# Router logits taken out of bursts and into the last walk of a feed-forward, in a fused attention and two-feed-forward kernel

## The chip, the cores and the metric

The kernel runs on one core of a Trainium2 chip. The metric is device time in microseconds (us) of one execution; lower is better. Three runs of the kernel before gave 2235.82, 2237.16 and 2239.37 us, with the median at 2237.16.

## What is computed

```python
# 1. attention: q, k, v of [4, 8, 576, 64], masked by blocks of 64, softmax, times v
x = attn.transpose(0, 2, 1, 3).reshape(2304, 512)
# 2. first feed-forward, d_ff 1536
xn = x / rms(x) * rms_g
x = (silu(xn @ w_gate) * (xn @ w_val)) @ w_out
# 3. second feed-forward, E = 8 experts of width 1024
logits = x @ gate                      # [2304, 8]
P = exp(logits - logits.max())
for _ in range(8):                     # the "normalisation"
    P /= P.sum(1, keepdims=True) + 1e-9
    P /= P.sum(0, keepdims=True) + 1e-9
    P *= 2304 / 8
out = sum(P[:, e:e+1] * (relu(x @ w1[e]) @ w2[e]) for e in range(8))
```

Everything is float32. The large products are made of three fp32r matmuls each (high times high, high times low, low times high part), so operands are split beforehand: a copy rounds to the high part, a subtraction gives the low part.

## The kernel before

**Order of the work.** The kernel does not issue instructions as it is written. Each piece of work is recorded with `G.op` (engine, estimated duration, function, buffers read and written, priority). `Graph.emit` then schedules all of it: 12 rounds of a forward list schedule and a backward pass that gives each piece its time to the end as its next key, and the round with the earliest estimated end is issued. `lat` is the delay that the scheduler assumes from a piece to those that depend on it. Splits, copies and additions may have a second engine (`alts`), which the scheduler chooses between. So a change in one place can change keys, engines and order anywhere else. Real waits come from the buffers alone, not from the estimates.

**Attention** (lines 370 to 870) makes 32 heads; the first feed-forward's first blocks of tokens are scheduled in among them. Line 662 (ScalarE) or its alternative on line 664 (VectorE) divides the probabilities by their sums.

**First feed-forward** (`moe1`, `moe1_up`, `moe1_down`). Tokens form five blocks of 512, 512, 512, 384 and 384 (`BL`); a pass over the 12 pieces of d_ff for one block is called a walk here. For each piece `xw` (matmuls of line 896) gives gate and value, ScalarE, VectorE and GpSimdE make the hidden tile, and for each two pieces line 927 multiplies by `wo` into the result `acc[j]`, added up by VectorE (line 936). The token operands of a walk lie in the two `XT` tiles in turn; the two `T1` tiles hold temporaries of every piece.

**Second feed-forward** (`moe2`). `logits(j)`, line 1140, multiplies each 128 tokens of `acc[j]` by the gate, whose right side has only 8 columns: 4 float32 matmuls for each of 18 token tiles, recorded as 144 TensorE instructions since each runs as two. One block's logits are one piece of work, in the one PSUM bank of the ring `PO`, copied out to `lg` by ScalarE. `sink` makes P out of them: VectorE sums rows, TensorE sums over partitions with a matmul by ones (line 1182), VectorE scales columns, eight times over. `pass_operands` makes the token operands of the first pass, a Strassen-like scheme over `acc[0]` to `acc[2]`: differences of blocks (helper `add`, line 1062) into the ring `CT`, then splits (lines 294, 298 and 307) into the tiles `xs` and, for the 256-token part, into one `XT` tile. `CT` begins with the two `T1` tiles, which are free only when the first feed-forward is done, and goes on with four pieces of the tile `pad`. `up` and `down` are the products with w1 (line 1279) and w2 (line 1344); each expert has four groups `g`, and for the first expert P is not needed. `first_pass` runs the logits, the operands, and then the groups; `sink` stands after the first group.

Of the kernel before, what the change touches and what calls it, by code (L numbers as in the profile page):

```python
# [226 lines left out]
def t_mm(n):  # L227
    return max(n / 2.4, 107.0) + 2
# [7 lines left out]
def tile_attn_moe_moe2(ctx: ExitStack, tc: tile.TileContext, qT, kT, vP, wg, wv, wo, rg, gw, w1, w2, ident_d, mq_d, mk_d, bm_d, out):  # L236
# [651 lines left out]

    THREE = ((0, 0), (0, 1), (1, 0))
# [13 lines left out]
    def moe1_up(j, f, wgt, wvt, prio):  # L903
# [3 lines left out]
        xw(psg, wgt, x1[j], xv, n, 2.0)  # L907
        xw(psv, wvt, x1[j], xv, n, 2.0)
# [32 lines left out]
    def moe1():  # L941
        batches = attention()
        pend = None
        for j in range(NB):
            next(batches, None)
            for g in range(NF // 2):
# [9 lines left out]
                for f in fs:  # L956
                    a = get("g", f, wg[f])
                    b = get("v", f, wv[f])
                    hs.append(moe1_up(j, f, a, b, 2.0))
# [5 lines left out]

    GF = 2
    NG = NF2 // GF
    c_pool = []

    def late(make):  # L970

        box = []

        def get():
            if not c_pool:
                att_stack.close()
                c_pool.append(ctx.enter_context(tc.tile_pool(name="c1", bufs=1, side="right", reuse_waits="tile")))
            if not box:
                box.append(make(c_pool[0]))
            return box[0]  # L980

        return get

    def late_buf(make, par=False):
        b = Buf(late(make), par=par)
        b.before = set(att_ops)
        return b
# [28 lines left out]
    def moe2():  # L1016
# [12 lines left out]
        def cut(o, n):  # L1029
# [14 lines left out]
        gwr = late_buf(lambda p: p.tile([128, NK, E], F32, name="gwr"))  # L1044
        onec = late_buf(lambda p: p.tile([128, 128], F32, name="onec"))
        lg = late_buf(lambda p: p.tile([128, TT, E], F32, name="lg"), par=True)
# [18 lines left out]

        read_x = {(j, p): set() for j in range(NB) for p in range(2)}
# [62 lines left out]
        G.op("SP", 100, lambda: nc.sync.dma_start(out=gwr(), in_=gw), w=[gwr], lat=2000)  # L1129
        G.op("DVE", 100, lambda: nc.vector.memset(onec(), 1.0), w=[onec])  # L1130

        def logits(j):

            n, nt, t0 = BL[j], BL[j] // 128, B0[j] // 128
            ps = PO.next()

            def go():
                for t in range(nt):
                    for k in range(NK):
                        nc.tensor.matmul(out=ps()[:, E * t : E * t + E], lhsT=raw_x(j, 128 * t, k, 128), rhs=gwr()[:, k, :],  # L1140
                                         start=k == 0, stop=k == NK - 1)

            o = G.op("PE", 220 * NK * nt, go, r=[gwr, *accb[j]], w=[ps], prio=1.0)
            read_x[j, 0].add(o)
            read_x[j, 1].add(o)
            G.op("ACT", 150, lambda: nc.scalar.activation(
                out=lg()[:, t0 : t0 + nt, :], in_=ps()[:, 0 : E * nt].rearrange("p (t e) -> p t e", t=nt), func=AF.Copy),
                r=[ps], w=[lg])

        def sink():  # L1150

            V = nc.vector
            G.op("DVE", 300, lambda: V.tensor_reduce(out=sc1()[:, 0:1], in_=lg().rearrange("p t e -> p (t e)"), axis=AX, op=ALU.max),
                 r=[lg], w=[sc1])
# [458 lines left out]
```

## Time and profile before

| what | value |
|---|---|
| median of three runs | 2237.16 us |
| the profiled execution, its own time | 2237.22 us |
| its span, first to last instruction | 2234.7 us |
| TensorE busy | 2182.5 us, 98% of the span |
| VectorE, ScalarE, GpSimdE busy | 1467.0, 990.3, 1148.5 us |
| mean granted TensorE clock | 0.984 |

The span covers the instructions of the core; 2.5 us of the execution's time lie outside it. The granted clock is a share of full speed: 1.00 is 2.4 GHz and 0.50 is 1.2 GHz, and a value between is a stretch in which both occurred. Busy time of TensorE includes slow matmuls, so 98% busy does not mean 98% at full speed. In the tables PE is TensorE, PEld its weight loads, DVE VectorE, ACT ScalarE, POOL GpSimdE and SP the engine that issues the DMAs.

### The profile page before, as it was taken

What the parts mean: (1) busy time and instruction counts of PE and PEld (TensorE: products, weight loads), DVE (VectorE), ACT (ScalarE), POOL (GpSimd) and SP (SyncE); (2) the same over time, 40 slices, a digit from 0 to 9 for tenths busy, and PEclk for the clock granted to TensorE, in tenths of its full rate; (3) what the DMA queues carried; (4) which work ended last, traced back from release to release, by engine and by line L of the source; (5) the groups of instructions that cost most, each with busy time, mean ns of one, the idle gap of its engine ahead of it and who ended that gap; (6) DMA issues with size and microseconds to landing.
All of it is one profiled execution on the core that took longest, in us unless ns stands there. A gap on an engine that the chain in (4) does not pass through costs nothing.

```text
span 2234.7 us, 31371 instructions
## 1 busy us (share of the span) xinstructions
PE 2182.5 (98%) x10974; PEld 1870.0 (84%) x10974; DVE 1467.0 (66%) x2455; ACT 990.3 (44%) x2134; POOL 1148.5 (51%) x1050
## 2 busy tenths in 40 slices
PE   8798899999999999999999999999999999999999
PEld 6676678887899989999999999999888888888887
DVE  7889967666632577655555555555667777777665
ACT  6789667575311354333343333344342323233332
POOL 6456732321411565556656565565465546454554
PEclk9699999999999999999999999999999999999999
DMA  6556666553677455554555555455565566656563
GB/s 166 178 169 201 192 231 217 164 162 114 208 252 228 142 176 193 192 190 170 176 182 189 184 190 183 170 173 186 202 222 192 188 206 197 196 190 209 192 202 113
DMA packets 159025, 418.16 MB, mean 187 GB/s; under 512 B 22282, under 2 KB 50762, under 8 KB 158868
## 3 DMA queue, kind: packets, MB, share of 16 engines
q1 hardware_dynamic: 158868, 416.17, 56.2%
q8 instruction: 86, 1.41, 0.3%
q14 instruction: 71, 0.58, 0.1%
HBM read 275.00 MB, written 141.08 MB: 186 GB/s over the span
## 4 chain that ended last, share of the span: by engine, by line
PE 84%; DVE 4%; ACT 1%; issue 1%; POOL 0%; DVEq 0%; POOLq 0%; ACTq 0%
PE ps L1279 24%; PE pm L1344 19%; PE pm L1501 11%; PE pm L896 10%; PE pm L1279 7%; PE pm L927 5%; PE po L1501 3%; PE ps L672 1%; PE ps L487 1%; PE po L715 1%; PE po L1140 1%; DVE acc L356 0%; DVE acc L354 0%; DVE qa L461 0%; DVE acc L936 0%
## 5 line engine op out<-in xcount | busy, mean ns | idle before, releaser
L1279 PE MATMUL ps<-xs,w 128*128 128x384 f32 (+2 forms) x2478 | 508.3, 348 | 2.2 <-ACT xs L294 1.3
L1279 PEld LDWEIGHTS ps<-xs,w 128*128 128x128 f32 x2478 | 437.8, 189 | 47.8 <-ACT xs L294 1.7
L896 PE MATMUL pm<-x,w 128*128 128x512 f32 (+1 forms) x1440 | 335.7, 379 | 2.8 <-POOL w L307 1.3
L1359 DVE SCALAR_TENSOR_TENSOR acc<-pm,Pm,acc 128x512 f32<-128x512 f32 x280 | 210.0, 750 | 156.5 <-PE pm L1344 153.6
L896 PEld LDWEIGHTS pm<-x,w 128*128 128x128 f32 x1440 | 260.6, 192 | 35.3 <-POOL w L307 2.4
L1344 PE MATMUL pm<-w,h 128*128 128x512 f32 x1152 | 279.6, 391 | 0.0
L307 POOL TENSOR_TENSOR w<-raw,w 128x512 fp32r<-128x512 f32 (+1 forms) x156 | 194.2, 1254 | 126.7 <-ACT w L294 114.0
L1344 PEld LDWEIGHTS pm<-w,h 128*128 128x128 f32 x1152 | 210.2, 188 | 39.3
L1344 PE MATMUL pm<-w,x 128*128 128x512 f32 x768 | 187.4, 392 | 0.0
L307 POOL TENSOR_TENSOR h<-t,h 128x512 fp32r<-128x512 f32 (+1 forms) x61 | 74.4, 1219 | 199.9 <-ACT h L294 179.4
L1344 PEld LDWEIGHTS pm<-w,x 128*128 128x128 f32 x768 | 143.0, 188 | 26.7
L927 PE MATMUL pm<-h,w 128*128 128x512 f32 (+1 forms) x720 | 163.9, 374 | 1.0 <-DVE h L307 0.5
L1482 DVE TENSOR_TENSOR acc<-pm,acc 128x512 f32<-128x512 f32 x169 | 116.5, 690 | 68.7 <-PE pm L1501 68.0
L927 PEld LDWEIGHTS pm<-h,w 128*128 128x128 f32 x720 | 129.7, 190 | 18.1 <-DVE h L307 1.0
L1279 PE MATMUL pm<-xs,w 128*128 128x256 f32 (+2 forms) x654 | 139.1, 336 | 0.0
L1293 DVE TENSOR_TENSOR pad<-ps,pad 128x384 f32<-128x384 f32 (+2 forms) x127 | 66.2, 522 | 104.6 <-ACT pad L1288 65.6
L1501 PE MATMUL pm<-x,w 128*128 128x512 f32 x510 | 126.5, 391 | 0.5 <-DVE x L307 0.5
L307 POOL TENSOR_TENSOR x<-pad,x 128x512 fp32r<-128x512 f32 (+1 forms) x71 | 92.3, 1302 | 67.4 <-ACT x L294 64.0
L1279 PEld LDWEIGHTS pm<-xs,w 128*128 128x128 f32 x654 | 111.9, 189 | 15.0
L1288 ACT ACTIVATE pad<-ps 128x256 f32<-128x256 f32 (+2 forms) x115 | 55.0, 478 | 145.1 <-PE ps L1279 145.0
L1288 ACT ACTIVATE t<-ps 128x384 f32<-128x384 f32 (+1 forms) x72 | 36.3, 504 | 181.8 <-PE ps L1279 179.1
L307 POOL TENSOR_TENSOR w<-pad,w 128x512 fp32r<-128x512 f32 x62 | 85.6, 1383 | 60.1 <-ACT w L294 55.6
(352 smaller groups left out, 4282.8 us busy)
## 6 DMA issues: line engine op xcount, KB each, us to landing
raw<-w_dram SPq DMA_DIRECT2D x128, 256.0 KB, 2.9
w<-kg SPq DMA_DIRECT2D x48, 512.0 KB, 4.4
w<-kv SPq DMA_DIRECT2D x48, 512.0 KB, 3.9
w<-ko SPq DMA_DIRECT2D x48, 512.0 KB, 4.2
fa<-w SPq DMA_DIRECT2D x32, 512.0 KB, 4.1
fd<-w SPq DMA_DIRECT2D x32, 512.0 KB, 3.9
sb<-w SPq DMA_DIRECT2D x32, 512.0 KB, 3.8
sc<-x SPq DMA_DIRECT2D x32, 512.0 KB, 2.6
```

Of the source, the lines that this page charges most:

```text
L307: eng.tensor_tensor(out=out_(), in0=a(), in1=b(), op=ALU.subtract)
L487: nc.tensor.matmul(out=ps()[:, o : o + n], lhsT=a[:, 128 * t : 128 * t + 128], rhs=c[:, k0 : k0 + n], start=start, stop=stop)
L672: A("PE", 109 if n > 64 else 58, lambda: nc.tensor.transpose(out=ps()[:, o : o + n], in_=p()[0:n, k0 : k0 + 128], identity=ident_t[0:n, 0:n]),
L896: nc.tensor.matmul(out=ps()[:, 0:n], lhsT=w()[:, a, 128 * k : 128 * k + 128], rhs=xv()[:, c, k, 0:n], start=k == 0 and (a, c) == (0, 0), s ...
L927: nc.tensor.matmul(out=ps()[:, 0:n], lhsT=wos[q]()[:, a, 128 * m : 128 * m + 128], rhs=ht()[:, c, 0:n], start=q == 0 and (a, c) == (0, 0), ...
L1279: nc.tensor.matmul(out=bank()[:, 0:n], lhsT=w()[:, a, o + 128 * k : o + 128 * k + 128], rhs=views[p, q, i, k, c](), start=start and k == 0 ...
L1288: G.op("ACT", t_act(n, True), lambda: nc.scalar.activation(out=t()[:, 0:n], in_=bank()[:, 0:n], func=AF.Copy), r=[bank], w=[t])
L1293: G.op("DVE", t_v1(n), lambda: nc.vector.tensor_tensor(out=t()[:, 0:n], in0=bank()[:, 0:n], in1=t()[:, 0:n], op=ALU.add), r=[bank, t], w=[t])
L1344: nc.tensor.matmul(out=y(), lhsT=hs[f][half]()[:, a, o : o + 128], rhs=ws[f]()[:, c, :], start=f == 0 and (a, c) == (0, 0), stop=f == GF - ...
L1359: G.op("DVE", 63 + t_v1(512), lambda y=y, dst=dst, tt=tt, e=e: nc.vector.scalar_tensor_tensor(out=dst(), in0=wide(y()), scalar=Pm()[:, tt, ...
L1482: G.op("DVE", t_v1(N), lambda: nc.vector.tensor_tensor(out=dst(), in0=bank()[:, 0:N], in1=dst(), op=ALU.add), r=[bank, dst], w=[dst])
L1501: nc.tensor.matmul(out=bank()[:, 0:N], lhsT=w()[:, a, o : o + 128], rhs=ops[i][gi]()[:, c, 0:N], start=start and gi == 0 and (a, c) == (0, ...
```

## The change

Three things are changed. First, the router's gate is loaded and its PSUM bank taken at the start of the last walk, and the logits are made one matmul group at a time: 60 of the 72 (15 token tiles by 4) stand between the gate and value products of the last walk, from its second piece on; the other 12, of the last block, stand two at a time in the first group's 256-token product. One ScalarE copy takes all of them to `lg`. Second, the first pass's operands are recorded before the rest of `moe2` and use a ring `CT0` of eight pieces of `pad`, without the `T1` tiles. Third, in `sink` the assumed delays between VectorE and TensorE are 2000 ns and 300 ns in place of 130 ns and its VectorE estimates are longer, and the products with w2 of the first expert's last group are made to come, in the scheduler, after the last scaling of `sink`.

```diff
-    def xw(ps, w, x, xv, n, prio):
+    def xw(ps, w, x, xv, n, prio, more=()):
         for k in range(NK):
-            def go(k=k):
+            extra = more[k] if more else []
+            def go(k=k, extra=extra):
                 for a, c in THREE:
                     nc.tensor.matmul(
...
+                for t, k2 in extra:
+                    logit(t, k2)
-            G.op("PE", 3 * t_mm(n), go, r=[w, x[k]], w=[ps], prio=prio)
+            o = G.op("PE", 3 * t_mm(n) + 260 * len(extra), go, r=[w, x[k], *logit_reads(extra)], w=[ps, *logit_writes(extra)], prio=prio)
+            logit_done(o, extra)
...
+    def logit(t, k):
+
+        j = max(x for x in range(NB) if B0[x] <= 128 * t)
+        o = k * BL[j] + 128 * t - B0[j]
+        nc.tensor.matmul(out=router["ps"]()[:, E * t : E * t + E], lhsT=acc[j][:, o : o + 128], rhs=router["gw"]()[:, k, :],
+                         start=k == 0, stop=k == NK - 1)
...
         for j in range(NB):
             next(batches, None)
+            spots = [[] for _ in range(NF * 2 * NK)]
+            if j == NB - 1:
+                router["gw"] = late_buf(lambda p: p.tile([128, NK, E], F32, name="gwr"))
+                router["ps"] = PO.next()
+                G.op("SP", 100, lambda: nc.sync.dma_start(out=router["gw"](), in_=gw), w=[router["gw"]], lat=2000)
+                todo = [(t, k) for t in range(B0[j] // 128) for k in range(NK)]
+                first = 2 * NK
+                for i, x in enumerate(todo):
+                    spots[first + i * (len(spots) - first) // len(todo)].append(x)
...
-        CT = ring_of([*T1.tiles, *(cut(3072 + 384 * i, 384) for i in range(4))],
-                     [set().union(*(b.users for b in T1[-2:]))] * 2 + [atts] * 4)
-        SP_ = ring_of([cut(512 * i, 512) for i in range(4)], [atts] * 4)
+        CT0 = ring_of([*(cut(3072 + 384 * i, 384) for i in range(4)), *(cut(512 * i, 512) for i in range(4))], [atts] * 8)
...
+        xs0 = pass_operands(0, CT0)
+        diffs = atts.union(*(b.users for b in CT0))
+        CT = ring_of([*T1.tiles, *(cut(3072 + 384 * i, 384) for i in range(4))],
+                     [set().union(*(b.users for b in T1[-2:]))] * 2 + [diffs] * 4)
+        SP_ = ring_of([cut(512 * i, 512) for i in range(4)], [diffs] * 4)
...
-        def logits(j):
...
         def sink():
...
+            SLACK, BACK = 2000.0, 300.0
...
             for _ in range(8):
-                G.op("DVE", 1424, rows, r=[Pm], w=[Pm, sm1, sm8])
+                G.op("DVE", 1950, rows, r=[Pm], w=[Pm, sm1, sm8], lat=SLACK)
...
-                     r=[onec, sm8], w=[pc])
-                G.op("DVE", 665, lambda pc=pc: columns(pc), r=[pc, Pm], w=[Pm, sc1])
+                     r=[onec, sm8], w=[pc], lat=BACK)
+                last = G.op("DVE", 800, lambda pc=pc: columns(pc), r=[pc, Pm], w=[Pm, sc1], lat=SLACK)
...
+            return last
...
-                        G.op("PE", 3 * GF * t_mm(512), go, r=[hs[0][half], hs[1][half], *ws], w=[y], prio=2.0)
+                        G.op("PE", 3 * GF * t_mm(512), go, r=[hs[0][half], hs[1][half], *ws], w=[y], prio=2.0,
+                             after=early if (e, g) == (0, 3) else ())
...
-            for j in range(NB):
-                logits(j)
-            xs = pass_operands(0, CT)
+            xs = xs0
+            rest = [(t, k) for t in range(B0[NB - 1] // 128, TT) for k in range(NK)]
...
-                        hs = up(0, q, xs[q], w1s, CT, relu)
+                        hs = up(0, q, xs[q], w1s, CT, relu, rest if q else None)
...
-                        sink()
+                        early.add(sink())
```

`up` takes two entries of `rest` ahead of each of its products, as `xw` takes `more`; both record the tokens read, so that `acc` is not overwritten before. Lines move by 24 to 30 numbers: 896, 927, 1140, 1182, 1279 and 1344 of before are 920, 976, 935, 1202, 1304 and 1372 of the change.

**TensorE in the last walk.** The rows below are TensorE's order before, where the logits of the first block (`gwr` is the gate, `acc_61` the first block) come between two pieces; pm is the PSUM tile, x_84 the walk's tokens, w a weight tile, and x16 counts logit matmuls in a row.

```order
L927 MATMUL pm_89<-h_78,w_74 128x384 x3
L927 MATMUL pm_89<-h_79,w_66 128x384 x3
L1140 MATMUL po_96<-gwr,acc_61 128x8 x16
L896 MATMUL pm_90<-x_84,w_69 128x384 x12
L896 MATMUL pm_91<-x_84,w_70 128x384 x12
```

The same place with the change, from the walk's second piece on:

```order
L920 MATMUL pm_90<-x_84,w_69 128x384 x3
L935 MATMUL po_96<-gwr,acc_61 128x8
L920 MATMUL pm_90<-x_84,w_69 128x384 x3
L935 MATMUL po_96<-gwr,acc_61 128x8
L920 MATMUL pm_90<-x_84,w_69 128x384 x6
L935 MATMUL po_96<-gwr,acc_61 128x8
```

Sixteen logit matmuls in a row have become single ones, each between groups of three or six wide matmuls, and this pattern goes on through the walk.

**TensorE at the first rounds of `sink`.** Before, these are the rows from the matmul that spreads the maximum (line 1159) to the second matmul by ones (line 1182); xs and x_85 are token operands, sm the row sums.

```order
L1159 MATMUL po_96<-sc_6556,onec 128x1
L1279 MATMUL ps_93<-xs_5334,w_69 128x384 x6
L1182 MATMUL po_96<-sm_6609,onec 128x8
L1279 MATMUL ps_94<-xs_5291,w_69 128x256 x3
L1279 MATMUL ps_94<-x_85,w_69 128x256 x3
L1279 MATMUL ps_93<-xs_5280,w_70 128x384 x6
L1279 MATMUL ps_93<-xs_6510,w_68 128x384 x6
L1182 MATMUL po_96<-sm_6609,onec 128x8
```

With the change (1179 and 1202 are those two lines; 1372 is the product with w2):

```order
L1179 MATMUL po_96<-sc_6725,onec 128x1
L1304 MATMUL pm_92<-xs_5262,w_73 128x384 x6
L1304 MATMUL ps_95<-xs_5291,w_66 128x384 x6
L1304 MATMUL ps_93<-xs_5282,w_66 128x384 x6
L1372 MATMUL pm_89<-w_71,x_84 128x512 x3
L1372 MATMUL pm_89<-w_72,x_84 128x512 x3
L1304 MATMUL ps_95<-xs_5311,w_67 128x384 x6
L1372 MATMUL pm_90<-w_71,x_84 128x512 x3
L1372 MATMUL pm_90<-w_72,x_84 128x512 x3
L1202 MATMUL po_96<-sm_6805,onec 128x8
```

Ahead of the first matmul by ones stood 6 wide matmuls; now 36 stand there (24 of 384 columns, 12 of 512).

**VectorE in the attention.** This is a piece of the difference, around the normalisation of one head (rs holds the inverse sums, p the probabilities; lines 354 and 356 convert weights).

```order
-L664 TENSOR_SCALAR p_1_120<-p_1_120,rs_135 128x256
-L354 TENSOR_SCALAR acc_64<-acc_64 128x512
-L664 TENSOR_SCALAR p_1_126<-p_1_126,rs_135 128x576
-L356 SCALAR_TENSOR_TENSOR acc_64<-acc_64 128x512
-L911 SCALAR_TENSOR_TENSOR t_83<-t_83,pm_90 128x512
-L664 TENSOR_SCALAR p_1_122<-p_1_122,rs_135 128x384
```

These multiplications have left VectorE for ScalarE. Counted over the whole order, line 664 has 12 rows before and 5 now, and line 662 has 113 and 120. The attention's order differs in many places; after the first groups of `moe2` the order on TensorE is the same again to the end.

## Rows read from the trace of the kernel before

**Rows 1.** The page: TensorE's busy tenths and clock in 40 slices, and the final chain.

```profile
PE   8798899999999999999999999999999999999999
...
PEclk9699999999999999999999999999999999999999
...
PE 84%; DVE 4%; ACT 1%; issue 1%; POOL 0%; DVEq 0%; POOLq 0%; ACTq 0%
```

**Rows 2.** Chain of waits, 690 to 830 us: start us, us, what.

```profile
696.46 8.32 PE pm L896 x48
...
708.94 3.47 PE po L1140 x32
712.41 9.99 PE pm L896 x48
...
730.04 10.01 PE pm L896 x48
...
748.37 3.47 PE po L1140 x32
...
756.10 2.58 PE po L1140 x24
...
759.82 4.10 PE po L1140 x24
763.92 3.86 PE ps L1279 x12
...
826.47 2.09 PE ps L1279 x12
```

**Rows 3.** Windows of 2 us: us, busy PE, PEld, DVE, ACT, POOL, PEclk, DMA share, GB/s.

```profile
710.00:712.00 2.00, 2.00 (x20) 2.00 (x19) 0.00 (x0) 0.00 (x0) 0.00 (x0) 1.00 0.93 346
...
714.00:716.00 2.00, 2.00 (x8) 2.00 (x7) 0.00 (x0) 0.00 (x0) 0.00 (x0) 0.50 0.00 0
...
752.00:754.00 2.00, 2.00 (x13) 2.00 (x12) 0.56 (x1) 0.89 (x3) 2.00 (x3) 1.00 0.89 318
```

**Rows 4.** Timeline of TensorE after 768 us: start, us, instruction, idle before and releaser.

```profile
772.16 0.39 PE L1182 MATMUL po<-sm,onec 128*128 128x8 f32 x2 [1.87 <-DVE sm L1170]
...
775.07 1.31 PE L1279 MATMUL ps<-xs,w 128*128 128x384 f32 x6 [0.64 <-ACT pad L1288]
776.82 0.39 PE L1182 MATMUL po<-sm,onec 128*128 128x8 f32 x2 [0.44 <-DVE sm L1170]
```

**Rows 5.** Chain of waits again, 780 to 830 us, around single matmuls by ones.

```profile
785.70 0.12 PE po L1182 x2
785.83 1.16 PE pm L1279 x6
...
802.81 0.12 PE po L1182 x2
802.93 1.48 PE pm L1344 x6
...
822.65 1.39 PE pm L1344 x6
824.04 1.04 PE ps L1279 x6
```

**Rows 6.** Windows in the attention, columns as in rows 3.

```profile
78.00:105.00 27.00, 19.59 (x73) 15.74 (x74) 21.16 (x50) 19.16 (x47) 11.61 (x9) 0.50 0.68 204
...
160.00:170.00 10.00, 9.79 (x39) 7.60 (x39) 7.19 (x15) 8.27 (x20) 3.54 (x4) 0.67 0.39 101
120.00:300.00 180.00, 160.50 (x740) 121.96 (x740) 169.04 (x292) 142.01 (x329) 118.14 (x96) 0.95 0.64 203
```

**Rows 7.** Groups of instructions by line, VectorE: busy us and mean ns.

```profile
L664 DVE TENSOR_SCALAR p<-p,rs 128x576 f32<-128x576 f32 (+4 forms) x12 | 8.0, 670 | 0.0
```

**Rows 8.** Windows at the start of `sink` and in the walks, columns as in rows 3.

```profile
768.00:778.00 10.00, 6.98 (x43) 5.78 (x42) 9.23 (x26) 5.42 (x14) 8.49 (x14) 1.00 0.24 94
600.00:700.00 100.00, 100.00 (x579) 100.00 (x578) 41.32 (x78) 21.96 (x49) 21.36 (x25) 1.00 0.77 253
```

More of the change, by code (lines that the diff above doesn't have):

```diff
@@ L886, in attention, with late, get, late_buf @@
                     yield
+    GF = 2
+    NG = NF2 // GF
+    c_pool = []
+    def late(make):
+        box = []
+        def get():
+            if not c_pool:
+                att_stack.close()
+                c_pool.append(ctx.enter_context(tc.tile_pool(name="c1", bufs=1, side="right", reuse_waits="tile")))
+            if not box:
+                box.append(make(c_pool[0]))
+            return box[0]
+        return get
+    def late_buf(make, par=False):
+        b = Buf(late(make), par=par)
+        b.before = set(att_ops)
+        return b
     THREE = ((0, 0), (0, 1), (1, 0))
-    def xw(ps, w, x, xv, n, prio):
+    def xw(ps, w, x, xv, n, prio, more=()):
         for k in range(NK):
-            def go(k=k):
+            extra = more[k] if more else []
+            def go(k=k, extra=extra):
                 for a, c in THREE:
@@ L898, in go, with logit_reads, logit_writes, logit_done @@
                         start=k == 0 and (a, c) == (0, 0), stop=k == NK - 1 and (a, c) == (1, 0))
-            G.op("PE", 3 * t_mm(n), go, r=[w, x[k]], w=[ps], prio=prio)
+                for t, k2 in extra:
+                    logit(t, k2)
+            o = G.op("PE", 3 * t_mm(n) + 260 * len(extra), go, r=[w, x[k], *logit_reads(extra)], w=[ps, *logit_writes(extra)], prio=prio)
+            logit_done(o, extra)
+    router = {}
+    read_x = {(j, p): set() for j in range(NB) for p in range(2)}
+    def logit(t, k):
[3 more added lines that the diff above has]
+                         start=k == 0, stop=k == NK - 1)
+    def logit_reads(extra):
+        return [router["gw"], *(accb[max(x for x in range(NB) if B0[x] <= 128 * t)][k] for t, k in extra)] if extra else []
+    def logit_writes(extra):
+        return [router["ps"]] if extra else []
+    def logit_done(o, extra):
+        for t, k in extra:
+            j = max(x for x in range(NB) if B0[x] <= 128 * t)
+            read_x[j, 0].add(o)
+            read_x[j, 1].add(o)
     accb = [[fixed(acc[j][:, m * BL[j] : (m + 1) * BL[j]]) for m in range(4)] for j in range(NB)]
-    def moe1_up(j, f, wgt, wvt, prio):
+    def moe1_up(j, f, wgt, wvt, prio, more=((), ())):
         n = BL[j]
@@ L906, in moe1_up @@
         psg, psv, t1, ht = PM.next(), PM.next(), T1.next(), HT.next()
-        xw(psg, wgt, x1[j], xv, n, 2.0)
-        xw(psv, wvt, x1[j], xv, n, 2.0)
+        xw(psg, wgt, x1[j], xv, n, 2.0, more[0])
+        xw(psv, wvt, x1[j], xv, n, 2.0, more[1])
         G.op("ACT", t_act(n, True), lambda: nc.scalar.activation(out=t1()[:, 0:n], in_=psg()[:, 0:n], func=AF.Tanh, scale=0.5),
@@ L963, in moe1 @@
         moe1_down(*pend)
[L966 to L987, printed above, removed]
     def ring_of(tiles_, before):
@@ L1128, in moe2 @@
         views = {}
-        G.op("SP", 100, lambda: nc.sync.dma_start(out=gwr(), in_=gw), w=[gwr], lat=2000)
-        G.op("DVE", 100, lambda: nc.vector.memset(onec(), 1.0), w=[onec])
-        def logits(j):
[L1134 to L1148, printed above, removed]
+        xs0 = pass_operands(0, CT0)
@@ L1158, in sink @@
+            G.op("DVE", 200, lambda: V.tensor_reduce(out=sc1()[0:1, 1:2], in_=ps()[0:1, 0:128], axis=AX, op=ALU.max), r=[ps, sc1], w=[sc1], lat=SLACK)
             pb = PO.next()
             G.op("PE", 400, lambda: nc.tensor.matmul(
-                out=pb()[:, 0:1], lhsT=onec()[0:1, :], rhs=sc1()[0:1, 1:2], start=True, stop=True), r=[onec, sc1], w=[pb])
+                out=pb()[:, 0:1], lhsT=onec()[0:1, :], rhs=sc1()[0:1, 1:2], start=True, stop=True), r=[onec, sc1], w=[pb], lat=BACK)
             G.op("DVE", 70, lambda: V.tensor_scalar_mul(out=sc1()[:, 2:3], in0=pb()[:, 0:1], scalar1=-1.0), r=[pb, sc1], w=[sc1])
@@ L1263, in reload, with up @@
             return out
-        def up(p, q, xs, ws, CT, finish):
+        def up(p, q, xs, ws, CT, finish, more=None):
             n = WIDTH[p][q]
@@ L1274, in m @@
                 first.add(bank)
+                extra = [more.pop(0) for _ in range(2) if more]
                 def go():
+                    for t, k in extra:
+                        logit(t, k)
                     for k in range(2):
@@ L1282, in go @@
                                 skip_group_check=not start)
-                G.op("PE", 6 * t_mm(n), go, r=[w, *xs[i]], w=[bank], prio=2.0)
+                o_ = G.op("PE", 6 * t_mm(n) + 260 * len(extra), go, r=[w, *xs[i], *logit_reads(extra)], w=[bank, *logit_writes(extra)], prio=2.0)
+                logit_done(o_, extra)
             def keep(bank):
```

15 lines of the change are left out of this document (8 added, 7 removed).

## The prediction

> **What bounds the kernel now.** The page comes first [rows 1]. TensorE is busy for 90% or more of nearly every slice after the first three, and it is 84% of the chain that ended last, so only time taken out of TensorE's own row shortens the kernel: slow clock, waits, or work. The clock row has one 6 in the first three slices and then 9s. A mean over a slice of 56 us hides short falls, so the stretch that the change touches, the last walk and the start of the second feed-forward (672 to 830 us), is read in the chain of waits [rows 2] and in windows of 2 us [rows 3].
>
> There the reader should compare equal pieces of work. Forty-eight wide matmuls of a walk take 8.32 us. The same 48 behind the first logit burst take 9.99 us, and behind the second 10.01 us [rows 2]. The windows say why: at 710 to 712 us, inside the burst, the granted clock is 1.00, at 714 to 716 us it is 0.50, which is 1.2 GHz, with TensorE busy for all of both windows [rows 3]. What the engine did before the fall was 32 matmuls of 8 columns, 3.47 us in all [rows 2]. The third burst, also 3.47 us [rows 2], is followed by a clock of 1.00 [rows 3], so a burst does not always bring a fall. The fourth and fifth stand close together: 24 matmuls take 2.58 us in one and 4.10 us in the other, and the 12 wide ones after it take 3.86 us where 12 of the same kind take 2.09 us later [rows 2].
>
> The other loss in this stretch is waiting. Between 768 and 778 us TensorE is busy for 6.98 of 10 us while VectorE is busy for 9.23 and GpSimdE for 8.49; in the walks it is busy for 100 of 100 us and those two for 41 and 21 [rows 8]. The timeline names the waits: 1.87 and 0.44 us for the row sums of the normalisation, 0.64 us for a bank that ScalarE has to empty [rows 4].
>
> **Term 1, the bursts go.** What is lost to the slow clock is 1.67 (9.99 less 8.32), 1.69, 1.52 (4.10 less 2.58) and 1.77 us (3.86 less 2.09) [rows 2], 6.65 us in sum. In the order of the change no two logits stand together in the last walk, each has 3 or 6 wide matmuls on both sides, and the 12 of the last block come as pairs among matmuls of 256 columns. Single narrow matmuls in such company exist before: the matmuls by ones of line 1182 stand among wide ones after 780 us [rows 5], and those that follow them run at full speed (1.16 us for six where six alone take 1.04 us, which leaves no room for half speed). So I take all of it: **-6.65 us**. The ends are 0 and -6.65.
>
> **Term 2, what a spread logit costs.** The logits are not fewer. In a burst one logit, two matmuls with their weight loads, costs 3.47 / 16 = 0.217 us [rows 2]. Alone between wide matmuls the pair of line 1182, of the same shape, takes 0.12 us and makes the six behind it longer: 1.16 against 1.04 us, in sum 0.24 us, or 1.48 against 1.39 us, in sum 0.21 us [rows 5]. The first has neighbours of 384 columns as in the walk, so I take 0.24 for the 60 that are spread: 60 x 0.023 = **+1.4 us**. With 0.21 it is -0.4, with 0.24 for all 72 +1.7. The gate's DMA and its place in SP's queue cost nothing: it is issued once, as before, and the whole first piece of the walk lies between it and the first logit. The single copy to `lg` replaces five and is off TensorE's path until `sink`.
>
> **Term 3, the waits at `sink`.** Before, 6 wide matmuls (1.04 us) stood ahead of the first matmul by ones and TensorE waited 1.87 us more [rows 4, 5], so VectorE and ScalarE needed about 2.9 us. The order now has 36 wide ones there: 24 x 8.32 / 48 [rows 2] and 12 x 1.39 / 6 [rows 5], 6.9 us. Later rounds have as much or more. So 1.87 and 0.44 us go, **-2.3 us**. The 0.64 us for the bank I leave, since the bank is still filled and emptied in the same way. What fills VectorE and GpSimdE there, the operands' differences and splits, has moved to the start of the fourth walk and to the end of it, where VectorE has 59 of 100 us free and GpSimdE 79 [rows 8]; that is their cover. Were it gone, the hidden tile would be late and TensorE would stand as it did at 772 us. The waits then range from 0 (all 2.95 us gone) to 2.95 (others in the same place). The later products with w2 of the fourth group are only ordered after `sink`: no semaphore is added, and nothing waits for it.
>
> **Term 4, the attention.** It is not edited, but the order differs there. From 120 to 300 us VectorE is busy for 169 of 180 us and TensorE for 160.5, at a mean clock of 0.95 [rows 6]: VectorE sets the pace. Seven normalisations go from VectorE to ScalarE, which has 38 of the 180 us free; at 0.670 us each [rows 7] that is 4.7 us less on VectorE. Other swaps of copies and subtractions between the engines go both ways. The gain is at most -4.7 us. At the other end a different order can make TensorE's clock fall once more, as at 160 to 170 us, where 10 us at 0.67 lose 3.3 us [rows 6]. I take **-1.0 us**, a little on the gaining side of the middle, since VectorE is the fuller engine.
>
> **Sum.** -6.65 + 1.4 - 2.3 - 1.0 = -8.55 us against the profiled execution's own 2237.22 us, which is 0.06 us over the median of the runs: **2228.7 us**, -0.38%. With its terms' nearer ends (term 4 from -4.7 to +1, term 3 from -2.95 to -1) this case reaches from 2224 to 2232.5.
>
> **Rivals.**
> - *The waits move instead of going.* The operands that now fill the start of the fourth walk hold back its hidden tiles, or weights of the first expert are late at 760 us. For it: the same operands fill both engines at 768 us [rows 8]. Against: the walk's free shares [rows 8]. It gives back the 2.3 us: 2231.0 us. Chance 0.10.
> - *The clock falls all the same.* Then term 1 is 0 and the time 2235.3 us. For it: one of the bursts brought no fall [rows 2, 3], so bursts alone are not the whole cause. Against: every fall in these rows came inside a burst or right behind one. The Trainium skill, "TensorE: Matmul & The Clock Gate", section "Part 1: The HAM clock gate", says that idleness throttles the clock and that a busy engine keeps it at full speed; by that rule, read by busy time, the bursts would not be the cause and 2235.3 us would come out. The rows disagree: 2.00 of 2.00 us busy and 0.50 granted [rows 3]. Chance 0.12.
> - *The attention loses a little.* One more fall like that at 160 us, +3.3 us in place of -1.0: 2233.0 us. Chance 0.10.
> - *The attention loses much: slower than before.* From 78 to 105 us the clock is 0.50 all through, with TensorE busy for 19.6 of 27 us [rows 6]. If the new order's waits bring another such stretch where TensorE is nearly full, 27 us of work at half speed cost 13.5 us: 2228.7 + 1.0 + 13.5 = 2243.2 us. It decides from 13.1 us on, which is 26 us of slow clock more. Against: the same pieces of work, and a lighter VectorE. Chance 0.08.
>
> **How the numbers follow.** The forecast has 0.60. About 0.2%, 4.5 us, is what a measurement of this kernel tells from no change; so 2232.7 and 2241.7 are the bounds. Faster: the forecast and the moved waits, 0.70. Same: the falling clock and the small loss in the attention, 0.22. Slower: 0.08. The range from 2223 to 2236 takes in all but the slow case and the forecast's outer ends, a little under 2 in 10.
>
> **What would show it.** Right: no logit row longer than single matmuls between 670 and 760 us; a clock of 1.00 in all windows there; 48 wide matmuls with their logits in 8.32 us and 0.24 us for each of their 10 or 11 logits; no TensorE wait for the row sums; and TensorE busy for over 9.5 of the 10 us after `sink` begins. Up to the start of the fourth walk the two traces should differ by less than 5 us. Wrong: a clock under 1.00 in the last walk, a wait for h or w there, or a start of the fourth walk that moved by more than the end did.

## The result and the profile after

The changed kernel takes 2213.86 us (median of 4 runs, 2212.94 to 2214.94); the kernel before 2238.08 us (4 runs: the three given above and one more). The ratio is 0.9893, 95% interval 0.9876 to 0.991: faster by 24 us. The forecast was 2228.7 us with a range from 2223 to 2236, so the sign was right and the size was not: the time lies 9 us below the range. The profiled execution has a span of 2211.4 us (before 2234.7), 23.3 us less, and that difference can be split by place. Three lines mark the places: the first of ScalarE's copies of `acc` in the fourth walk (taken below as the walk's beginning), the last products with w2 in the first pass, and the last upward products of the second pass. The rows give the first and the last start of each. Before:

```profile
L933 ACT ACTIVATE acc<-pm x8: 472/493/494, 606.7 to 684.0; 128x384 f32<-128x384 f32 x8
...
L1344 PE MATMUL pm<-w,h x1152: 387/389/476, 784.2 to 1601.1; 128*128 128x512 f32 x192
...
L1501 PE MATMUL pm<-x,w x510: 387/389/497, 1653.1 to 2220.5; 128*128 128x512 f32 x170
```

After, the same operations (columns: operation, count, ns min/median/max, first to last start in us, shape):

```profile
L982 ACT ACTIVATE acc<-pm x8: 492/492/493, 597.7 to 678.2; 128x384 f32<-128x384 f32 x8
...
L1372 PE MATMUL pm<-w,h x1152: 387/389/478, 761.5 to 1582.7; 128*128 128x512 f32 x192
...
L1529 PE MATMUL pm<-x,w x510: 387/389/505, 1634.4 to 2197.2; 128*128 128x512 f32 x170
```

| stretch | before | after | difference | forecast |
|---|---|---|---|---|
| attention and first walks, up to 606.7 / 597.7 | 606.7 | 597.7 | -9.0 | -1.0 |
| last walks, logits, `sink`, first pass, up to 1601.1 / 1582.7 | 994.4 | 985.0 | -9.4 | -7.55 |
| second pass, up to 2220.5 / 2197.2 | 619.4 | 614.5 | -4.9 | 0 |
| end | 14.2 | 14.2 | 0 | 0 |

Nine of the 23.3 us come from a stretch that the change does not edit, and five from another.

The page shows it less sharply. Its clock row has a 7 where it had a 6 [rows 1], and TensorE's share of the chain that ended last rose from 84% to 88%:

```profile
PEclk9799999999999999999999999999999999999999
...
PE 88%; DVE 6%; ACT 2%; issue 1%; DMA 1%; POOL 1%; SPq 0%; DVEq 0%; POOLq 0%; ACTq 0%
```

In the edited stretch the chain of waits shows the spread logits at work. The 48 wide matmuls that took 8.32 us alone and 9.99 or 10.01 us behind a burst [rows 2] now run from 708.10 to 718.80 us with 11 logits among them:

```profile
708.10 0.52 PE pm L920 x3
708.62 0.12 PE po L935 x2
708.74 0.62 PE pm L920 x3
...
709.49 1.15 PE pm L920 x6
...
718.68 0.12 PE po L935 x2
718.80 0.80 PE pm L976 x4
```

That is 10.70 us, 2.38 more than 8.32, or 0.216 us for a logit. In a burst it was 0.217. Three windows that answer to earlier ones follow (columns: us, then busy time of PE, PEld, DVE, ACT and POOL, PEclk, DMA share, GB/s):

```profile
120.00:300.00 180.00, 162.66 (x759) 124.33 (x758) 164.99 (x291) 141.94 (x335) 120.23 (x96) 0.96 0.63 200
768.00:778.00 10.00, 10.00 (x51) 8.68 (x50) 3.13 (x10) 3.98 (x8) 5.91 (x8) 1.00 0.48 176
...
714.00:716.00 2.00, 2.00 (x15) 2.00 (x14) 0.00 (x0) 0.53 (x1) 1.01 (x1) 1.00 0.73 250
```

At 714 us the clock is 1.00 where it was 0.50 [rows 3], and at 768 us TensorE is busy for 10.00 of 10 us where it was 6.98 [rows 8], while VectorE fell from 9.23 to 3.13. In the attention, from 120 to 300 us, VectorE has 165.0 us in place of 169.0 [rows 6]. From 600 to 850 us the list of TensorE's waits is empty, so those of [rows 4] are gone, the 0.64 us for the bank too.

### The profile page after: what moved, and what is told of

It reads as the page before. It is cut to its first block, busy times and chain, and to the rows that moved or that the text cites. A ratio compares the mean times of both kernels' runs of the same rounds, so it can differ in the third digit from the quotient of the medians.

```text
span 2211.4 us, 31378 instructions
## 1 busy us (share of the span) xinstructions
PE 2167.9 (98%) x10974; PEld 1861.2 (84%) x10974; DVE 1424.4 (64%) x2408; ACT 987.4 (45%) x2134; POOL 1194.0 (54%) x1093
## 4 chain that ended last, share of the span: by engine, by line
PE 88%; DVE 6%; ACT 2%; issue 1%; DMA 1%; POOL 1%; SPq 0%; DVEq 0%; POOLq 0%; ACTq 0%
PE ps L1304 24%; PE pm L1372 20%; PE pm L920 11%; PE pm L1529 11%; PE pm L1304 7%; PE pm L976 6%; PE po L1529 3%; PE ps L487 2%; PE ps L672 2%; PE po L715 1%; DVE mn L496 1%; DVE acc L356 1%; ACT p L662 1%; DVE qa L461 1%; DVE acc L354 0%
## 5 line engine op out<-in xcount | busy, mean ns | idle before, releaser
L920 PE MATMUL pm<-x,w 128*128 128x512 f32 (+1 forms) x1440 | 344.1, 379 | 2.4 <-POOL w L307 1.4
L920 PEld LDWEIGHTS pm<-x,w 128*128 128x128 f32 x1440 | 254.6, 190 | 36.0 <-POOL w L307 3.4
L307 POOL TENSOR_TENSOR h<-t,h 128x512 fp32r<-128x512 f32 (+1 forms) x64 | 80.2, 1254 | 196.7 <-ACT h L294 166.7
L307 POOL TENSOR_TENSOR x<-pad,x 128x512 fp32r<-128x512 f32 (+1 forms) x75 | 99.4, 1328 | 58.4 <-ACT x L294 58.3
L1529 PEld LDWEIGHTS pm<-x,w 128*128 128x128 f32 x510 | 95.7, 188 | 20.9 <-DVE x L307 0.9
```

Source lines behind the costliest of these rows:

```text
L307: eng.tensor_tensor(out=out_(), in0=a(), in1=b(), op=ALU.subtract)
L920: nc.tensor.matmul(out=ps()[:, 0:n], lhsT=w()[:, a, 128 * k : 128 * k + 128], rhs=xv()[:, c, k, 0:n], start=k == 0 and (a, c) == (0, 0), s ...
L1529: nc.tensor.matmul(out=bank()[:, 0:N], lhsT=w()[:, a, o : o + 128], rhs=ops[i][gi]()[:, c, 0:N], start=start and gi == 0 and (a, c) == (0, ...
```

## The experiments

**How a place is held.** The planner reorders the whole program at any edit. To change one thing at a time, several kernels hold a region to the order and the engine choices that another kernel's plan had there: a table of numbers, walked when the work is issued. Two regions are used: the 3901 operations ahead of the last walk ("attention's order"), and the last 1904 ("second pass's order"). These operations are the same in both kernels; only order and engine differ. All kernels were run for five rounds beside the kernel before; the first four on one chip, the next four on a second, the last four on a third.

```diff
+HELD = [
+    (0, 3901, "..."),
...
+]
...
-        for fn in best[1]:
+        for fn in out:
             fn()
```

The table gathers what all runs gave. "To walk 4", "middle" and "second pass" are the first three stretches of the table above, from each kernel's profiled execution.

| kernel | median us | ratio to before, interval | to walk 4 | middle | second pass |
|---|---|---|---|---|---|
| before | 2238.08 | 1 | 606.7 | 994.4 | 619.4 |
| after | 2213.86 | 0.9893 (0.9876 to 0.991) | 597.7 | 985.0 | 614.5 |
| e1 after, old attention's order | 2222.47 | 0.9927 (0.9915 to 0.994) | 607.6 | 984.5 | 614.5 |
| e2 before, new attention's order | 2232.11 | 0.9965 (0.9952 to 0.9979) | 599.5 | 1001.6 | 621.1 |
| e3 before, new second pass's order | 2235.7 | 0.9993 (0.9984 to 1.0002) | 607.9 | 997.7 | 616.9 |
| e4 before, tenth round | 2230.17 | 0.9965 (0.9953 to 0.9978) | 597.4 | 999.5 | 616.7 |
| e5 after, bursts back | 2220.18 | 0.9921 (0.9909 to 0.9934) | 597.3 | 989.6 | 614.5 |
| e6 after, old ring | 2228.51 | 0.9964 (0.9952 to 0.9976) | 597.6 | 997.4 | 616.2 |
| e7 after, old `sink` | 2216.88 | 0.991 (0.9896 to 0.9923) | 598.3 | 985.2 | 614.8 |
| e8 before, spread alone | 2238.1 | 1.0002 (0.9993 to 1.0011) | 607.4 | 998.0 | 616.8 |
| e9 before, own tiles alone | 2231.54 | 0.9969 (0.9958 to 0.9981) | 606.2 | 991.1 | 616.8 |
| e10 after, 60 rounds | 2214.98 | 0.9895 (0.9881 to 0.9908) | 601.0 | 983.4 | 615.1 |
| e11 after, twelfth round | 2221.29 | 0.9926 (0.9912 to 0.9939) | 602.7 | 984.0 | 614.2 |
| e12 before, eleventh round | 2237.7 | 1.0001 (0.9992 to 1.001) | 602.4 | 1003.0 | 618.9 |

The ratio is to the runs of before made beside each kernel; their medians were 2237.23, 2237.54 and 2238.27 us on the three chips. The profiled execution is not always a middling one: that of e2 was the longest of its five (2238.25 us), that of e3 the second longest of its eleven (2239.13 us), that of e9 the shortest of its six (2230.33 us).

**Does the attention's gain lie in its order? (e1, e2)** The edit is the table above, with `before`'s order in the changed kernel, and the other way round.

> The changed kernel, with the order and the choice of engine that the planner gave the kernel before for everything ahead of the last walk (attention, its normalisation and the first four walks, 3901 planned operations); the last walk, the hand-over and both passes stay as changed. Theory A (the 9 us gained ahead of the last walk come from another order of the same operations): about 2223 us, and the last walk begins near 681 us in place of 675. Rival B (those 9 us do not hang on that order, but on the last walk or on the run): about 2214 us and 675 us.

> The kernel before, with only the order and the choice of engine that the planner gave the changed kernel for the 3901 operations ahead of the last walk; logits in bursts, tiles, waits and passes as before. Theory A (order alone): about 2229 us, the last walk begins some 9 us earlier, and everything behind it takes as long as before. Rival B (the order gains only together with the edits): about 2238 us.

In e1 the nine us go back: 607.6 us to the fourth walk, and 2222.47 us, 8.6 more than the changed kernel. The middle and the second pass stay as changed, 984.5 and 614.5 us. Theory A stands. The other kernels that have one of the two orders agree: with the old one (before, e1, e3, e8, e9) the fourth walk begins at 606.2 to 607.9 us, with the new one (after, e2, e5, e6, e7) at 597.3 to 599.5. In e2 the fourth walk begins 7.2 us sooner than before, as it should, but the time falls by 5.1 us only, and in the profiled execution the middle, whose order was not touched, takes 1001.6 us in place of 994.4. The windows show the cause (TensorE alone: us, busy, PEclk, DMA share, GB/s). Before:

```profile
0.00:120.00 120.00, 98.33 (x431) 0.83 0.60 167
120.00:310.00 190.00, 170.50 (x789) 0.96 0.62 195
670.00:790.00 120.00, 116.98 (x697) 0.94 0.54 180
```

After:

```profile
0.00:120.00 120.00, 101.45 (x451) 0.86 0.61 171
120.00:310.00 190.00, 172.66 (x811) 0.96 0.64 206
670.00:790.00 120.00, 120.00 (x740) 1.00 0.60 207
```

e2, the kernel before with the new attention's order:

```profile
0.00:120.00 120.00, 101.28 (x453) 0.87 0.61 172
...
670.00:790.00 120.00, 117.36 (x659) 0.87 0.50 165
```

Ahead of 310 us the changed kernel's TensorE idles 35.9 us where it idled 41.2 (310 less the busy sums), 5.3 us less. In the first 120 us its clock is 0.86 in place of 0.83, which is about 3.6 us more of full-speed work (0.03 x 120, an estimate, since this mean counts idle time too). Together that is about the 9.0 us. In the hand-over from 670 to 790 us e2's clock is 0.87 where the kernel before had 0.94 with the same bursts: 8.4 us more lost (0.07 x 120, an estimate of the same kind). TensorE's order there is the same in both, and so it is in e3.

**Is that order the change's own? (e4, e10 to e12)** e4 and e12 are the kernel before with another of the planner's rounds, e11 the changed kernel so; in e10 the changed kernel has more rounds to choose from.

```diff
-            if best is None or end < best[0]:
+            if r == 9:
```

```diff
-ROUNDS = 12
+ROUNDS = 60
```

(In e12 the number is 10, and in e11, on the changed kernel, 11.)

> The kernel before without any edit of its work, but with the order of the planner's tenth round in place of the seventh, which it takes because its own estimate for it is the least (2028.05 us; 2028.49 us for the tenth, 0.02% more). Theory A (the order of attention is drawn anew by any edit, and what it costs on the chip the estimate does not see): the time moves by several us, to anywhere between 2226 and 2246 us, with the last walk's beginning moved alike. Rival B (the orders of two rounds are worth the same, so the change's better order is the change's own): within 2 us of 2238 us.

> The kernel before, no edit of its work, with the order of the planner's eleventh round (estimate 2028.48 us, where the seventh's is 2028.05). Theory A (the seventh's order was a bad draw, orders of other rounds are like the tenth's): the sums of the last head near 530 us and about 2230 us. Rival B (the tenth was a good draw): 538 us and 2237 us or more.

> The changed kernel with the order of the planner's last round (estimate 2026.6 us) in place of its tenth (2025.6 us). Theory A (the estimate decides): 2215 us. Rival B (an order drawn anew): 2210 to 2224 us, with the difference lying ahead of 310 us, as idle time of TensorE and as slow clock.

> The changed kernel with nothing altered but the number of the planner's rounds, 60 in place of 12; its best estimate falls from 2025.6 to 2021.2 us. Theory A (the estimate sees what the chip does): 4.4 us less, 2209.5 us. Rival B (an order drawn anew, worth what the slow clock in the attention makes of it): anywhere from 2208 to 2224 us, the start of the fifth walk moving alike.

e4 settles it. Without any edit the fourth walk begins at 597.4 us, as early as in the changed kernel, for a plan that the planner holds to be 0.02% worse, and the time falls by 7 us. Its windows:

```profile
0.00:120.00 120.00, 101.18 (x452) 0.87 0.62 172
120.00:310.00 190.00, 173.96 (x815) 0.96 0.65 206
670.00:790.00 120.00, 114.94 (x663) 0.91 0.53 180
```

They are the changed kernel's up to 310 us, but not behind. e12 gains 4.3 us up to the fourth walk and gives it all back in the hand-over (clock 0.86 from 670 to 790 us, 0.94 before). It comes out at 2237.7 us, so neither of its expectations held as put: the order of the attention was better than before, the time the same. e11 loses 5.0 us to the fourth walk and 7.4 us in all; e10 has an estimate that is 4.4 us better and a time that is 1.1 us longer. In all four the estimate was no guide to a few us. No version beat the changed kernel; e10, made in the hope of that, cannot be told from it.

The five kernels with an unedited hand-over (before, e2, e3, e4, e12) took 994.4, 1001.6, 997.7, 999.5 and 1003.0 us in the middle, each in one profiled execution; after, e1, e7 (which has the old `sink`), e10 and e11 took 985.0, 984.5, 985.2, 983.4 and 984.0. The first three have one order on TensorE there and still differ by 7.2 us, so not all of this scatter is the planner's: much of it changes from execution to execution. The profile that the forecast was made from had the cheapest hand-over of the five, and against the changed kernel's 985.0 us the edits are worth 9 to 18 us. The edited middle is steady to 1.8 us: its clock is 1.00 from 670 to 790 us in all five, and its waits there come to 0.2 us at most.

**What is the spread worth? (e5, e8)** In e5 `logits(j)` and the five copies come back, and the two lists are empty:

```diff
-                    spots[first + i * (len(spots) - first) // len(todo)].append(x)
...
-            rest = [(t, k) for t in range(B0[NB - 1] // 128, TT) for k in range(NK)]
+            rest = []
+            for j in range(NB):
+                logits(j)
```

In e8 the ring of e6 and the `sink` of e7 (below) are taken back together, and both regions keep the old order.

> The changed kernel with the logits in five bursts again, as before; attention and second pass keep the changed kernel's order. Theory A (the slow clock behind the bursts): TensorE's clock falls to 0.50 again in two to six places between 695 and 770 us, and since the fall's cost was 6.65 us in the profile of the kernel before and more in those of the runs so far (10 to 15 us of work at half speed), the time is 2219 to 2229 us and scatters more from run to run than the changed kernel's 2 us. Rival B (the hand-over gained by the operands and the waits, not by the clock): 2214 to 2216 us.

> The kernel before with only the logits spread over the last walk: old ring, old normalisation, and the old kernel's order in attention and second pass. Theory A (the spread removes the slow clock and a spread logit costs what one in a burst does, 0.217 us): 6.65 us by the profile of the kernel before, up to 10 us by the mean of the profiles with bursts, so 2227 to 2231 us, and a clock of 1.00 from 672 to 770 us. Rival B (the gain needs the other two edits): 2235 us or more. The waits for the row sums should still be there, 2 to 3 us.

e5 takes 2220.18 us, 6.3 more than the changed kernel, and its runs scatter over 6.2 us (2216.22 to 2222.39) where the changed kernel's scatter over 2.0. (That does not hold for bursts in general: e9 below, with bursts, scatters over 2.2 us in six runs, e6, without, over 7.6 in six.) Its chain of waits shows both levels of the clock around its bursts; the first and the third are shown:

```profile
662.75 3.47 PE po L1215 x32
666.22 10.02 PE pm L965 x48
...
698.02 4.03 PE po L1215 x32
702.04 11.02 PE pm L965 x48
```

The first is as before [rows 2]; behind the third the same 48 take 11.02 us, 2.70 more than 8.32. A window of 2 us there has TensorE busy throughout and the clock at 0.50:

```profile
704.00:706.00 2.00, 2.00 (x8) 0.50 0.00 0
```

Theory A stands in the cause and the time. The falls lie behind the first three bursts, from 666 to 707 us, mostly earlier than it put them, and there is none behind the last two. But e8, the spread alone, gives nothing: 2238.1 us, ratio 1.0002 with an interval from 0.9993 to 1.0011. Its clock is 1.00 up to 760 us, as theory A had it, but rival B has the time: the gain needs another of the edits. The next experiment shows which.

**What are the tiles of their own worth? (e6, e9)**

```diff
-        CT0 = ring_of([*(cut(3072 + 384 * i, 384) for i in range(4)), *(cut(512 * i, 512) for i in range(4))], [atts] * 8)
+        CT = ring_of([*T1.tiles, *(cut(3072 + 384 * i, 384) for i in range(4))],
+                     [set().union(*(b.users for b in T1[-2:]))] * 2 + [atts] * 4)
...
-        xs0 = pass_operands(0, CT0)
+        xs0 = pass_operands(0, CT)
```

e9 has the tiles but the bursts of e5 and the `sink` of e7, with the old order in both regions.

> The changed kernel with the first pass's operands made from the ring of the kernel before (two tiles that the walk still uses, and four others) in place of eight tiles of their own; all else as changed, attention and second pass in the changed kernel's order. Theory A (the tiles of their own take the operands out of the hand-over, and that is what ended the waits for the row sums): two waits or more of TensorE between 760 and 790 us, 1.5 to 3 us in all, about 2216 us. Rival B (the waits went by the order of the normalisation alone): none of them, 2214 us.

> The kernel before with only the tiles of their own for the first pass's operands: logits in bursts, old normalisation, the old kernel's order in attention and second pass. With spread logits the old ring cost 14.6 us. Theory A (the operands' chain of differences through the ring takes its time in either case, and the bursts covered it before: they were work that TensorE could do while the first banks of the pass could not be emptied): the tiles bring little while the bursts stand, at most the 2.95 us of waits and a shift of the bursts, 2233 to 2238 us. Rival B (the ring costs the same without the spread): 2223 us.

e6 takes 2228.51 us, 14.7 more than the changed kernel: twice what the spread is worth, and not by the waits for the row sums that theory A expected. Both theories missed it. The timeline of TensorE in e6 (start, us, instruction, idle before and its releaser):

```profile
750.54 1.23 PE L1347 MATMUL ps<-xs,w 128*128 128x384 f32 x6
757.56 2.29 PE L1347 MATMUL ps<-xs,w 128*128 128x384 f32 x6 [5.79 <-ACT t L1357]
760.42 2.29 PE L1347 MATMUL ps<-xs,w 128*128 128x384 f32 x6 [0.58 <-ACT t L1357]
```

After the first product of the first pass TensorE stands for 5.79 us until ScalarE has copied a bank to the tile `t` (`keep`, line 1357). That tile is the next of the ring `CT`, and the ring is still taken by the operands' differences, each of which waits for the splits of the one before. The chain of waits shows that line of small steps:

```profile
750.06 0.73 DVE xs L352
...
754.10 0.71 POOL t L1142
...
756.81 0.31 ACT x L339
757.12 0.40 ACT t L1357
```

The old ring begins with the two `T1` tiles, which are free only when the walks have made their last hidden tile, so this line of steps cannot begin earlier. And the idle time is paid twice, as windows of 4 us in e6 show:

```profile
754.00:758.00 4.00, 0.44 (x1) 0.73 0.33 131
758.00:762.00 4.00, 3.42 (x11) 0.50 0.00 0
762.00:766.00 4.00, 3.37 (x11) 0.50 0.47 174
```

Behind the wait the clock is 0.50 and the six matmuls take 2.29 us where the six ahead of it took 1.23. The middle is 12.4 us longer than the changed kernel's: TensorE idles for 7.0 us of it (113.00 of 120 us busy from 670 to 790 us), and the other 5.4 go to the slow clock (an estimate, by this difference). Here the rule that the Trainium skill gives in "TensorE: Matmul & The Clock Gate", section "Part 1: The HAM clock gate", and that spoke against the forecast, is what the trace shows: idleness throttles. It explains this fall and not the one at 704 us in e5, behind narrow matmuls and with TensorE busy for 2.00 of 2.00 us.

In the kernel before, the same line of steps ran beside the bursts: from 748.37 us on 3.47, 2.58 and 4.10 us of logits stood between the last products of the walk and the pass [rows 2]. They were TensorE's cover. The copy of the first bank to `t` came late there too, behind the same splits, 9.9 us after the start of its product at 758.53 us, but TensorE had the last burst and other products to do:

```profile
768.43 0.49 ACT L1288 ACTIVATE t<-ps 128x384 f32<-128x384 f32 x1 [2.67 <-DVE xs L307]
```

Taken out of there without the tiles, the logits bared it. The 0.64 us of [rows 4] is not what was left of this wait: it is a later one on the same operation, for a copy to `pad`, and e6 and e8 have it besides. e8 has the wait for the copy to `t` too, among its three longest from 560 to 900 us (waited for, us in total, times, longest):

```profile
PE ps L1347 <- ACT t L1357: 6.4, 2, 5.8
PE po L1245 <- DVE sm L1233: 1.0, 2, 0.7
PE ps L1347 <- ACT pad L1357: 0.6, 1, 0.6
```

The row sums cost it 1.0 us, less than the 2 to 3 us expected.

e9 has the cover and the tiles and takes 2231.54 us, 6.7 less than before, a little under the range of its theory A (2233 to 2238) and far from B: 3.3 us in the middle, 2.6 in the second pass. So in the middle the tiles are worth 3.3 us beside bursts, less than the scatter of that stretch with bursts, and 12.4 us beside spread logits (997.4 less 985.0).

**Did the waits go by the order of the normalisation? (e7)**

```diff
-            SLACK, BACK = 2000.0, 300.0
+            SLACK, BACK = 130.0, 130.0
...
-                             after=early if (e, g) == (0, 3) else ())
+                             after=())
```

with 1950 and 800 ns back to 1424 and 665.

> The changed kernel with the planner's old costs and delays for the normalisation of the router's weights and without its edge to the fourth group, so that its small matmuls follow closely again; all else as changed, attention and second pass in the changed kernel's order. Theory A (the waits went because the small matmuls were put off): waits for the row sums come back, about 2.3 us in all, about 2216 us. Rival B (VectorE and GpSimd are free of the operands by then, so that the sums are ready anyway): none over 0.3 us, 2214 us.

Its one TensorE wait between 750 and 900 us:

```profile
PE po L1247 <- DVE sm L1235: 0.2, 1, 0.2
```

The middle takes 985.2 us, 0.2 more than changed. So the waits do not come back, as rival B has it, but not for B's reason, because the small matmuls do not follow closely in this kernel. Between the matmul that spreads the maximum and the first matmul by ones stand 24 wide ones, 5.6 us of work (TensorE, then VectorE's row sums):

```profile
765.49 0.38 PE L1224 MATMUL po<-sc,onec 1*128 1x1 f32 x2
765.80 5.72 PE L1417 MATMUL pm<-w,h 128*128 128x512 f32 x24
771.36 0.28 PE L1247 MATMUL po<-sm,onec 128*128 128x8 f32 x2
...
768.73 0.43 DVE L1235 TENSOR_REDUCE sm<-Pm 128x8 f32<-128x144 f32 x1
```

Before, the same two ends were:

```profile
768.52 0.38 PE L1159 MATMUL po<-sc,onec 1*128 1x1 f32 x2
...
771.69 0.42 DVE L1170 TENSOR_REDUCE sm<-Pm 128x8 f32<-128x144 f32 x1
```

From the start of the spreading matmul to the end of the sums it takes 3.67 us in e7 and 3.59 us before: the sums are not ready sooner, there is more work ahead of them. e9 speaks against B as well. It has the tiles of their own and the old `sink`, and TensorE waits for the row sums three times:

```profile
PE po L1258 <- DVE sm L1246: 1.7, 3, 0.7
```

In e6, with the old ring and the new `sink`, no wait for them is listed. What the runs leave is theory A's cause, wide work ahead of the small matmuls; why the planner puts so much there in e7 with the old delays was not tried. The median of e7 is 3.0 us longer than the changed kernel's, but the intervals of the two ratios overlap. The profiled execution, which was the shortest of the four, shows no place for it: its middle and its second pass are the changed kernel's to 0.3 us.

**And the second pass? (e3)** TensorE's order there is the same in both kernels; 55 additions and differences changed engine.

> The kernel before, with only the second pass of the second feed-forward ordered as in the changed kernel: TensorE's order is the same there, what differs is which of VectorE and GpSimd does 55 additions and differences, and their place in the order. Theory A (the 5 us gained in the second pass come from operands that are ready in time): about 2233 us, and the 0.40 us waits ahead of the weight loads of the upward matmuls fall from 11 to 2 or so. Rival B (the gain there is handed on from the earlier stages, or is the clock's): 2238 us, and the 11 waits stay.

TensorE's weight loads before, 1640 to 2230 us (waited for, us in total, times, longest):

```profile
PEld pm L1501 <- issue: 4.3, 11, 0.4
```

and in e3:

```profile
PEld pm L1545 <- issue: 0.8, 2, 0.4
...
L1545 PE MATMUL pm<-x,w x510: 387/389/504, 1657.5 to 2222.5; 128*128 128x512 f32 x170
```

From the first to the last upward product (line 1545, which is 1501 before) it takes 565.0 us in place of 567.4, so the order is worth 2.4 of the 4.6 us by which the changed kernel's 562.8 is shorter. The median moved by 1.5 us, within what can be told from no change. The other half is small steps: in the kernel before, and in e3, some groups of six matmuls take 1.39 us that take 1.36 after. Before:

```profile
1800.41 1.39 PE ps L1279 x6
```

After:

```profile
1815.89 1.36 PE pm L1304 x6
```

e8 and e9, which have part of the changed code and the old order with its 11 waits, take 565.1 us, and e4, which has the old code and 2 such waits, 564.8. So this half goes with the code and not with the order. What in the code does it was not tried, and stays open.

## Why the prediction was wrong

- **Term 4, the attention: the step that failed.** "I take -1.0 us", between -4.7 and +3.3. It was -9.0 in the profile, and e1 shows 8.6 us of the time hanging on it. The bound of -4.7 came from VectorE's lightened row alone; what moved was TensorE's idle time (5.3 us) and its clock (about 3.6 us). More than that, the term was treated as a result of the change, with a middle a little on the gaining side, when it is a new draw of the planner: e4 has the same gain without an edit, e12 half of it. The range lacked this draw.
- **The second pass: the other step that failed.** The sum had no term for it. The order on TensorE was the same and the time was not: -4.9 us, of which 2.4 go with the order of the other engines and the weight loads that were no longer held up; the cause of the rest stays open.
- **Term 1: right in size, for a reason with a gap.** -6.65 us; e5 measures 6.3. The slow clock did go wherever the bursts went. But the same bursts, in the same order on TensorE, lost about 8.4 us more in e2, so 6.65 was one draw, and e8 shows that it is not to be had alone.
- **Term 2: too dear.** +1.4 us; the sixty logits cost 0.216 us each in place of 0.217, so nothing. The price of 0.24 us was taken from a single matmul pair of another line [rows 5]; the lower end of the term, -0.4, was the nearer.
- **Term 3: right, but for the bank.** -2.3 us, because 36 wide matmuls stand ahead of the first row sums. They took 7.06 us (772.14 to 779.20 us) for the 6.9 reckoned, and the waits went, 2.95 us with the bank's 0.64. The cause holds as far as the runs go: with the new `sink` no wait for the row sums is listed, not even in e6, whose operands are made late; with the old one there are 2.3 us before, 1.7 in e9, 1.0 in e8 and 0.2 in e7, where 24 wide matmuls stand ahead. Only the sentence that left the 0.64 us alone, "the bank is still filled and emptied in the same way", overlooked that it is emptied into a tile of the ring that was changed.
- **The tiles were costed at a cover** ("that is their cover") and never as a term. Without them the spread bares a wait of 5.8 us and the slow clock behind it; they are worth 14.7 us in e6, more than any other edit.
- **The rivals.** None came. The clock did not fall (1.00 from 670 to 790 us), no wait took the old one's place, and the attention gained. The test named for it, that the start of the fourth walk should move by less than 5 us, failed as a test should: it moved by 9.0. In the last rival the sum slipped: from 2228.7 + 1.0 us the bound of 2241.7 is reached with 12.0 us, not 13.1; nothing else hangs on it.

## What to carry to other kernels

Where a planner orders the work, run the unedited kernel with a few of its other orders first: here two of them moved the attention by 4 and 9 us. And profile it more than once: with one order on TensorE the hand-over differed by up to 7 us between profiled executions. Both are of the size of the edits' own gain, so a forecast needs that scatter in its range, and a test of an edit must hold the other places to one order and go by several runs. Before taking work off the busiest engine at a hand-over, ask what ran beside it: a long chain of small steps may be running under the work that is taken away, with hardly a wait to show for it, and once bared it costs its idle time and the slow clock behind it. Edits that make up for each other have to be tried together as well as alone: the spread alone gave nothing, and the tiles beside the other edits 14.7 us.

## What the runs showed of the hardware that was not expected

Identical bursts of 8-column matmuls bring a different loss in each execution: in before, e2 and e3, with one order on TensorE, the mean clock from 670 to 790 us was 0.94, 0.87 and 0.91 (0.91 and 0.86 in e4 and e12, with other orders). Behind such a burst the clock stood at 0.50 with TensorE busy for 2.00 of 2.00 us. A pair of 8-column float32 matmuls costs the same between wide ones as in a burst, 0.216 us a logit against 0.217, though its own row shows 0.12 us: the rest is in the wide ones behind it, 0.62 us for 0.52 with three and 1.15 us for 1.04 with six.
